# Fourier mixing and GEGLU: gate and value of every third late block in two TensorE passes each, with the mirrored gelu, the value add and the product issued a slot later

## The chip, the cores and the metric

One core of a Trainium2 chip. The time is that of one execution on the device, in microseconds, median of several. TensorE (PE), VectorE (DVE), ScalarE (ACT) and GpSimd (POOL) each work through a queue of their own in order, and wait for one another by semaphores. TensorE's sums go into the memory PSUM (tiles `ps_...` of the profile), from which DVE and ACT read them; tiles `..._sb` lie in SBUF, the core's other memory.

## The reference, cut to what matters

```python
X = np.fft.fft(np.fft.fft(x, axis=1), axis=2).real       # x: 8 x 3008 x 256
g, val = X @ w_gate, X @ w_val                           # 256 -> 1536
out = (0.5 * g * (1 + erf(g / sqrt(2))) * val) @ w_out   # 1536 -> 256
```

The real part of a transform of real data is mirrored: a row and its mirror row have the same part E and an odd part O of opposite sign. So with the products E and O of one row, its gate is E + O and that of the mirror row E - O. One column of E does not fit the halves and is added as a rank-one term: the row EB times a weight `yw`.

## The kernel before: the parts that matter

It goes through 288 blocks (8 batches, 3 chunks of 512, 512 and 481 tokens, 12 feature blocks `fc`). A turn of the loop is a **slot**: the first half of one block, the second half of the block before, and two pieces of the output product of the chunk before.

```python
def l1_gate(ci, fc):                       # three gate passes in all: E, O, then M = -2 O
    pg = psum("g")
    mm(pg, n, "g", "E", fs, E, True, False)
    mm(pg, n, "g", "O", fs, O, False, True)
    nc.scalar.activation(gl[:, 0, :n], pg[:, :n], AF.Gelu)          # row
def l1_gate2(ci, fc):                      # a slot later
    mm(pg, n, "g", "M", fs, O, False, True, skip_group_check=True)
    nc.scalar.activation(<gl[:, 1], mirrored>, pg[:, :n], AF.Gelu)  # mirror row
def l1_value(ci, fc):                      # two value passes: E, O
    mm(pv, n, "v", "E", fs, E, True, True)
    nc.vector.scalar_tensor_tensor(ve, EB, yw, pv, op0=mult, op1=add)
def l1_value2(ci, fc):                     # a slot later
    mm(pv, n, "v", "O", fs, O, False, True, skip_group_check=True)
    nc.vector.tensor_tensor(h[0], gl[0], pv, op=mult)
    nc.vector.scalar_tensor_tensor(<vv, mirrored>, ve, 2.0, pv, op0=mult, op1=subtract)
    nc.gpsimd.tensor_tensor(h[1], gl[1], vv, op=mult)
# ... one slot of the loop:
    G(i); g(i - 1); V(i); <output piece>; <input folds>; v(i - 1); <output piece>; <transform work>
```

(Cut and shortened.)

## Time and profile before

| before | |
|---|---|
| median of the runs beside the first result | 630.28 us (629.87 to 631.15) |
| span of the profiled run | 627.0 us |
| PE, DVE, POOL, ACT busy | 98%, 92%, 81%, 68% |
| one slot at 512 columns | 1.955 us |

"Busy" is the share of the span in which an engine has an instruction in work. PE's 98% says that it is hardly ever without work, and the chain says that it sets the time. The prediction below shows the page's lines and one slot of the timeline.

### The profile page before, as it was taken

What the parts mean: (1) busy time and instruction counts of PE and PEld (TensorE: products, weight loads), DVE (VectorE), ACT (ScalarE), POOL (GpSimd) and SP (SyncE); (2) the same over time, 40 slices, a digit from 0 to 9 for tenths busy, and PEclk for the clock granted to TensorE, in tenths of its full rate; (3) what the DMA queues carried; (4) which work ended last, traced back from release to release, by engine and by line L of the source; (5) the groups of instructions that cost most, each with busy time, mean ns of one, the idle gap of its engine ahead of it and who ended that gap; (6) DMA issues with size and microseconds to landing.
All of it is one profiled execution on the core that took longest, in us unless ns stands there. A gap on an engine that the chain in (4) does not pass through costs nothing.

```text
span 627.0 us, 12895 instructions
## 1 busy us (share of the span) xinstructions
PE 612.3 (98%) x4195; PEld 405.1 (65%) x4243; DVE 578.3 (92%) x941; ACT 428.4 (68%) x842; POOL 505.3 (81%) x510
## 2 busy tenths in 40 slices
PE   7999999999999999999999999999999999999997
PEld 3456666666666666666666666666666666666666
DVE  8689989999899999999999998999999999999992
ACT  6777677666776677667676677676676666666661
POOL 8399999989897998879997899969988655555651
PEclk8999999999999999999999999999999999999999
DMA  9961754536353353731645335633212322221123
GB/s 177 227 97 31 210 129 116 144 105 159 99 146 101 98 133 79 184 113 46 160 110 135 101 78 127 148 97 98 62 49 63 91 86 55 51 52 39 42 51 81
DMA packets 54217, 65.40 MB, mean 104 GB/s; under 512 B 7831, under 2 KB 49802, under 8 KB 51754
## 3 DMA queue, kind: packets, MB, share of 16 engines
q1 hardware_dynamic: 47222, 49.03, 30.6%
q0 software_dynamic: 6608, 15.29, 11.4%
q8 instruction: 33, 0.54, 0.4%
q10 hardware_dynamic: 320, 0.26, 0.2%
q14 instruction: 34, 0.28, 0.2%
HBM read 39.65 MB, written 30.17 MB: 111 GB/s over the span
## 4 chain that ended last, share of the span: by engine, by line
PE 93%; ACT 2%; issue 1%; DVE 1%; DMA 1%; POOL 1%; POOLq 0%; ACTq 0%
PE ps_o L749 38%; PE ps_g L660 28%; PE ps_v L660 19%; PE ps_dft L546 2%; PE ps_dft L582 2%; PE ps_o L820 1%; DMA Z_sb<-z 1%; PE ps_dft L443 1%; PE ps_dft L612 0%; ACT gelu_sb L676 0%; POOL h_sb L724 0%; POOL eo_sb L224 0%; DMA out_dram<-out_sb 0%; ACT gelu_sb L685 0%; PE ps_dft L749 0%
## 5 line engine op out<-in xcount | busy, mean ns | idle before, releaser
L724 POOL TENSOR_TENSOR h_sb<-gelu_sb,v_sb 128x512 bf16<-128x512 bf16 (+1 forms) x280 | 319.8, 1146 | 93.1 <-DVE v_sb L722 85.9
L749 PE MATMUL ps_o<-Wo_sb,h_sb 128*128 128x256 bf16 (+1 forms) x2232 | 334.9, 273 | 0.9 <-POOL h_sb L724 0.9
L749 PEld LDWEIGHTS <-h_sb 128*128 128x128 bf16 (+1 forms) x2304 | 228.7, 100 | 112.9 <-POOL h_sb L724 2.6
L676 ACT ACTIVATE gelu_sb<-ps_g 128x512 bf16<-128x512 f32 (+1 forms) x288 | 169.4, 588 | 98.6 <-PE ps_g L660 80.9
L660 PE MATMUL ps_g<-EO_sb,W_sb 128*128 128x512 bf16 (+1 forms) x817 | 228.5, 375 | 3.8 <-ACT gelu_sb L685 0.8
L704 DVE SCALAR_TENSOR_TENSOR ve_sb<-EB_sb,yw,ps_v 128x512 f32<-128x512 bf16 (+1 forms) x280 | 206.3, 737 | 25.9 <-PE ps_v L660 25.0
L660 PE MATMUL ps_v<-EO_sb,W_sb 128*128 128x512 bf16 (+1 forms) x575 | 213.7, 375 | 0.7 <-DVE W_sb L451 0.6
L720 DVE TENSOR_TENSOR h_sb<-gelu_sb,ps_v 128x512 bf16<-128x512 bf16 (+1 forms) x280 | 189.9, 678 | 1.1 <-ACT gelu_sb L685 0.7
L660 PEld LDWEIGHTS <-W_sb 128*128 128x128 bf16 x1440 | 137.2, 98 | 81.1 <-issue 1.8
L722 DVE SCALAR_TENSOR_TENSOR v_sb<-ve_sb,ps_v 128x512 f32<-128x512 f32 (+1 forms) x280 | 187.5, 670 | 0.0
L685 ACT ACTIVATE gelu_sb<-ps_g 128x512 bf16<-128x512 f32 (+1 forms) x288 | 168.7, 586 | 0.0
L769 ACT ACTIVATE out_sb<-ps_o 128x512 f32<-128x512 f32 x92 | 55.0, 598 | 35.7 <-PE ps_o L749 35.6
L224 POOL TENSOR_TENSOR eo_sb<-ab_sb 94x512 bf16<-94x512 f32 (+1 forms) x70 | 77.6, 1111 | 0.5
L549 ACT ACTIVATE S_sb<-ps_dft 96x512 bf16<-96x512 f32 x56 | 32.9, 588 | 14.0 <-PE ps_dft L546 13.9
L592 ACT ACTIVATE EO_sb<-ps_dft 128x512 bf16<-128x512 f32 (+1 forms) x44 | 26.0, 590 | 23.3 <-PE ps_dft L582 22.1
L217 POOL TENSOR_TENSOR ab_sb<-x_raw,x_raw 94x508 f32<-94x508 f32 (+1 forms) x30 | 33.0, 1100 | 0.0
L220 POOL TENSOR_TENSOR ab_sb<-x_raw,x_raw 94x508 f32<-94x508 f32 (+1 forms) x30 | 32.9, 1098 | 0.0
L546 PE MATMUL ps_dft<-eo_sb,G 94*96 94x256 bf16 x119 | 22.5, 274 | 0.2 <-POOL eo_sb L224 0.2
L158 POOL DMA_INDIRECT x_raw<-in_x_dram,idx x18 | 17.1, 948 | 2.9 <-issue 1.1
L582 PE MATMUL ps_dft<-TP,Z_sb 128*128 128x128 bf16 (+1 forms) x184 | 17.8, 218 | 0.0
L582 PEld LDWEIGHTS <-Z_sb 128*128 128x128 bf16 x192 | 14.6, 98 | 1.8 <-DVE Z_sb L534 0.6
L546 PEld LDWEIGHTS <-G 94*96 94x96 bf16 x119 | 13.0, 123 | 1.2 <-issue 0.4
(148 smaller groups left out, 166.2 us busy)
## 6 DMA issues: line engine op xcount, KB each, us to landing
out_dram<-out_sb SPq DMA_DIRECT2D x364, 64.0 KB
x_raw<-in_x_dram SPq DMA_DIRECT2D x10, 768.0 KB
Z_sb<-z SPq DMA_DIRECT2D x7, 768.0 KB
z<-S_sb SPq DMA_DIRECT2D x7, 576.0 KB
EB_sb<-yrow SPq DMA_DIRECT2D x14, 128.0 KB
z<-S_sb SPq DMA_DIRECT2D x7, 192.0 KB
x_raw<-in_x_dram SPq DMA_DIRECT2D x2, 640.0 KB
EB_sb<-yrow SPq DMA_DIRECT2D x7, 120.2 KB
```

The costliest lines, as they stand in the source:

```text
L224: eng.tensor_tensor(_sub(eo, [[C, nj], [1, 128]], j0 * C + g * 128), ab(0, 0, [[1, 128]]), ab(1, 0, [[1, 128]]), op=op)
L546: nc.tensor.matmul(ps[:96, q * C : (q + 1) * C], G[:, j, :], _sub(eo, [[1, C]], j * C), start=(j == js[0]), stop=(j == js[-1]))
L582: nc.tensor.matmul(ps[:, o : o + n], st["Z"][:, pair, g * 128 : g * 128 + 128], _sub(TP, [[1, n]], g * 128), start=True, stop=True)
L660: nc.tensor.matmul(ps[:, :n], W[nm, part][:, fs], src, start=start, stop=stop, **kw)
L676: nc.scalar.activation(gl[:, 0, :n], pg[:, :n], AF.Gelu)
L685: nc.scalar.activation(_sub(gl, [[-1, n]], TOK + n - 1), pg[:, :n], AF.Gelu)
L704: nc.vector.scalar_tensor_tensor(ve[:, :n], EB_bufs[b][:, c0 : c0 + n], yw[:, fc : fc + 1], pv[:, :n], op0=ALU.mult, op1=ALU.add)
L720: nc.vector.tensor_tensor(st["h"][:, fc, 0, :n], gl[:, 0, :n], pv[:, :n], op=ALU.mult)
L722: nc.vector.scalar_tensor_tensor(_sub(vv, [[-1, n]], n - 1), ve[:, :n], 2.0, pv[:, :n], op0=ALU.mult, op1=ALU.subtract)
L724: nc.gpsimd.tensor_tensor(st["h"][:, fc, 1, :n], gl[:, 1, :n], vv[:, :n], op=ALU.mult)
L749: nc.tensor.matmul(pso[:m, half], st["h"][:, fc, sign, h0 : h0 + m], Wo_sb[:, fc, :], start=(fc == 0 and not (first and sign)), stop=(fc = ...
L769: nc.scalar.activation(_sub(osb, [[1, 2 * C]], 0, part_num=m), pso[:m, :], AF.Copy)
```

## The change

Its intent is to use the time that POOL and ACT have free in the last sixty blocks (41% and 36% between 543 and 590 us) to take one pass from PE. In nineteen blocks (229, 232, ... 283) ACT copies twice the E product out of PSUM, before the O pass is added to it. The mirror row is then (2 E) - (E + O), a subtraction, and the M pass is not needed. In the diff `d` holds the gate of the mirror row while it is made. To keep DVE at three instructions a block, the value goes the same way: the copy takes the place of `ve`.

```diff
+APART = tuple(i for i in range(B * NS - 60, B * NS - 2) if i % 3 == 1)
+def e2_tile(): return work([128, TOK], FP32, "e2", 2, "e2_sb")       # two buffers
 def l1_gate:
+    if apart(ci, fc):
+        mm(pg, n, "g", "E", fs, E, True, True)
+        nc.scalar.activation(e2[:, :n], pg[:, :n], AF.Copy, scale=2.0)
+def l1_gate_odd:                                # same slot, after the first output piece
+    mm(pg, n, "g", "O", fs, O, False, True, skip_group_check=True)
+    nc.vector.scalar_tensor_tensor(d, EB, ywg, pg, op0=mult, op1=subtract)
+    nc.scalar.activation(gl[:, 0, :n], pg[:, :n], AF.Gelu)
+    nc.gpsimd.tensor_tensor(d, e2, d, op=add)                        # "gate add"
 def l1_value:
+    if apart(ci, fc):
+        nc.scalar.activation(e2[:, :n], pv[:, :n], AF.Copy, scale=2.0)  # "value copy"
 def l1_value2:
+    if apart(ci, fc):
+        nc.vector.scalar_tensor_tensor(<vv, mirrored>, EB, yw2, pv, op0=mult, op1=subtract)
+        def rest():
+            nc.scalar.activation(<gl[:, 1], mirrored>, d, AF.Gelu)
+            nc.gpsimd.tensor_tensor(vv, <e2, mirrored>, vv, op=add)  # "value add"
+            nc.gpsimd.tensor_tensor(h[1], gl[1], vv, op=mult)
+        late.append(rest)                       # issued in the next slot, behind v(i)
```

(Cut and shortened. Left out: the weights `ywg` and `yw2`, made once, and a fifth `v` buffer.)

More of the change, by code (lines that the diff above doesn't have):

```diff
@@ L134, in v_tile, with e2_tile @@
     def v_tile():
-        return work([128, TOK], FP32, "v", 4, "v_sb")
+        return work([128, TOK], FP32, "v", 5, "v_sb")
+    def e2_tile():
+        return work([128, TOK], FP32, "e2", 2, "e2_sb")
     def osb_tile():
@@ L245 @@
     one_h = const_pool.tile([1, 1], BF16)
-    yw = const_pool.tile([128, NFC], FP32)
+    yw, yw2, ywg = (const_pool.tile([128, NFC], FP32, name=f"yw_{i}") for i in range(3))
     NGP = NJ * NK
@@ L250 @@
     rd = work([128, 2 * NGP + NK], FP32, "Z", 1, "rd")
-    cf, cr, cd = (work([128, C], FP32, t, 4, f"small_{i}") for i, t in enumerate(("v", "v", "v")))
+    cf, cr, cd = (work([128, C], FP32, t, 5, f"small_{i}") for i, t in enumerate(("v", "v", "v")))
     tf, tr, td = (work([128, 128], FP32, t, 3, f"small_t{i}") for i, t in enumerate(("ve", "ve", "ve")))
@@ L477, in make_yw, with make_ywg @@
         return run
+    def make_ywg():
+        fcs = sorted({i % NFC for i in APART})
+        ps = psum("dft")
+        for fc in fcs:
+            nc.tensor.matmul(
+                ps[:, fc : fc + 1], W["g", "O"][0:1, fc * 128 : (fc + 1) * 128], one_h, start=True, stop=True)
+        for fc in fcs:
+            nc.scalar.activation(ywg[:, fc : fc + 1], ps[:, fc : fc + 1], AF.Copy, scale=2.0)
+        nc.vector.tensor_scalar(yw2, yw, 2.0, None, op0=ALU.mult)
     EO_bufs, EB_bufs = {}, {}
@@ L634, in tp_o @@
         return tp_e(b, gi, 1, engine)
+    NS = NG * NFC
+    APART = tuple(i for i in range(B * NS - 60, B * NS - 2) if i % 3 == 1)
     def store(b, gi, sub, sign, osb_half, queue):
@@ L654, in store @@
             (nc.sync if i else queue).dma_start(out=dst, in_=_sub(osb_half, [[1, C]], 0, part_start=p1, part_num=hi - lo))
+    late = []
     def ffn_work(b):
@@ L667, in cols_of, with apart @@
             return n, c0, E, O, cstate[ci], slice(fc * 128, (fc + 1) * 128)
+        def apart(ci, fc):
+            return b * NS + ci * NFC + fc in APART
         def l1_gate(ci, fc):
@@ L672, in run @@
                 pg = psum("g")
+                if apart(ci, fc):
+                    mm(pg, n, "g", "E", fs, E, True, True)
+                    e2 = e2_tile()
+                    nc.scalar.activation(e2[:, :n], pg[:, :n], AF.Copy, scale=2.0)
+                    st["ps"][fc] = [pg, gelu_tile(), e2]
+                    return
                 mm(pg, n, "g", "E", fs, E, True, False)
@@ L678, in l1_gate, with l1_gate_odd, run @@
             return run
+        def l1_gate_odd(ci, fc):
+            def run():
+                if not apart(ci, fc):
+                    return
+                n, c0, _, O, st, fs = cols_of(ci, fc)
+                pg, gl, e2 = st["ps"][fc][:3]
+                del st["ps"][fc][2]
+                mm(pg, n, "g", "O", fs, O, False, True, skip_group_check=True)
+                d = v_tile()
+                nc.vector.scalar_tensor_tensor(
+                    d[:, :n], EB_bufs[b][:, c0 : c0 + n], ywg[:, fc : fc + 1], pg[:, :n],
+                    op0=ALU.mult, op1=ALU.subtract)
+                nc.scalar.activation(gl[:, 0, :n], pg[:, :n], AF.Gelu)
+                nc.gpsimd.tensor_tensor(d[:, :n], e2[:, :n], d[:, :n], op=ALU.add)
+                st["ps"][fc][0] = d
+            return run
         def l1_gate2(ci, fc):
@@ L683, in run @@
                 pg, gl = st["ps"][fc][:2]
+                if apart(ci, fc):
+                    return
                 mm(pg, n, "g", "M", fs, O, False, True, skip_group_check=True)
@@ L702, in run @@
                 mm(pv, n, "v", "E", fs, E, True, True)
+                if apart(ci, fc):
+                    e2 = e2_tile()
+                    nc.scalar.activation(e2[:, :n], pv[:, :n], AF.Copy, scale=2.0)
+                    st["ps"][fc] += [pv, e2]
+                    return
                 ve = ve_tile()
@@ L711, in run @@
             def run():
-                n, _, _, O, st, fs = cols_of(ci, fc)
-                _, gl, pv, ve = st["ps"].pop(fc)
+                n, c0, _, O, st, fs = cols_of(ci, fc)
+                dg, gl, pv, ve = st["ps"].pop(fc)
                 if three(ci, fc):
@@ L721, in run @@
                 vv = v_tile()
+                if apart(ci, fc):
+                    nc.vector.scalar_tensor_tensor(
+                        _sub(vv, [[-1, n]], n - 1), EB_bufs[b][:, c0 : c0 + n], yw2[:, fc : fc + 1], pv[:, :n],
+                        op0=ALU.mult, op1=ALU.subtract)
+                    def rest():
+                        nc.scalar.activation(_sub(gl, [[-1, n]], TOK + n - 1), dg[:, :n], AF.Gelu)
+                        nc.gpsimd.tensor_tensor(vv[:, :n], _sub(ve, [[-1, n]], n - 1), vv[:, :n], op=ALU.add)
+                        nc.gpsimd.tensor_tensor(st["h"][:, fc, 1, :n], gl[:, 1, :n], vv[:, :n], op=ALU.mult)
+                    late.append(rest)
+                    return
                 nc.vector.scalar_tensor_tensor(
@@ L777, in ffn_work @@
             parts = {k: [f(ci, fc) for fc in range(NFC)] for k, f in (
-                ("G", l1_gate), ("V", l1_value), ("g", l1_gate2), ("v", l1_value2))}
+                ("G", l1_gate), ("O", l1_gate_odd), ("V", l1_value), ("g", l1_gate2), ("v", l1_value2))}
             subs = [nsub - 1, *range(nsub - 1)] if last(ci) else range(nsub)
@@ L874, in behind_first_gate @@
         tp_y(0, 0)()
-    NS = NG * NFC
     def plan():
@@ L894, in plan @@
             at(fill, s, f)
+        at(fill, 14, make_ywg)
         for i, f in enumerate(early):
@@ L972, in feed @@
                 two.pop(0)()
+            parts["O"][fc]()
             for f in pool.pop(i, []):
                 f()
+            ready = list(late)
+            late.clear()
             if before:
                 before[0]["v"][before[1]]()
+            for f in ready:
+                f()
             if two:
```

## The prediction

> **What bounds the kernel now.** I read the page from the top: busy shares first, then the forty slices, then the chain that ended last.
>
> ```profile
> PE 612.3 (98%) x4195; PEld 405.1 (65%) x4243; DVE 578.3 (92%) x941; ACT 428.4 (68%) x842; POOL 505.3 (81%) x510
> ...
> POOL 8399999989897998879997899969988655555651
> ...
> PE 93%; ACT 2%; issue 1%; DVE 1%; DMA 1%; POOL 1%; POOLq 0%; ACTq 0%
> ```
>
> TensorE holds 93% of the chain. POOL runs near full until the input folds are over, then falls to about half in the last slices. That hole is what the change spends. The changed blocks are numbers 229, 232, ... 283 of 288 (nineteen), and by counting the starts of the ve instruction (L704) in the timeline backwards they lie between 496 and 604 us. So I read that stretch by windows (columns: length, then busy time of PE, weight load, DVE, ACT, POOL; clock; DMA):
>
> ```profile
> 543.00:590.00 47.00, 46.68 (x309) 30.94 (x313) 46.99 (x73) 30.08 (x57) 27.94 (x25) 1.00 0.18 44
> 590.00:611.00 21.00, 21.00 (x146) 14.01 (x144) 20.91 (x34) 12.93 (x26) 12.44 (x12) 1.00 0.21 51
> ```
>
> PE and DVE are both full there, ACT and POOL have 36 to 41% free. One block in the timeline (start, length, engine):
>
> ```profile
> 559.66 0.38 PE L660 MATMUL ps_g<-EO_sb,W_sb 128*128 128x512 bf16 x1
> ...
> 559.88 0.38 PE L660 MATMUL ps_v<-EO_sb,W_sb 128*128 128x512 bf16 x1
> ...
> 560.29 0.75 DVE L704 SCALAR_TENSOR_TENSOR ve_sb<-EB_sb,yw,ps_v 128x512 f32<-128x512 bf16 x1
> 560.41 0.59 ACT L685 ACTIVATE gelu_sb<-ps_g 128x512 bf16<-128x512 f32 x1
> ...
> 560.49 1.16 POOL L724 TENSOR_TENSOR h_sb<-gelu_sb,v_sb 128x512 bf16<-128x512 bf16 x1 [0.79 <-DVE v_sb L722]
> 560.53 0.38 PE L660 MATMUL ps_v<-EO_sb,W_sb 128*128 128x512 bf16 x1
> ...
> 561.02 0.69 DVE L720 TENSOR_TENSOR h_sb<-gelu_sb,ps_v 128x512 bf16<-128x512 bf16 x1
> ...
> 561.62 0.68 DVE L722 SCALAR_TENSOR_TENSOR v_sb<-ve_sb,ps_v 128x512 f32<-128x512 f32 x1
> 561.83 0.38 PE L660 MATMUL ps_v<-EO_sb,W_sb 128*128 128x512 bf16 x1
> ```
>
> A slot lasts 1.955 us (the same value pass starts at 559.88 and 561.83). It holds nine times 0.217 us of PE: gate E, O and M, value E and O, and two output pieces of four 256-column passes, each piece worth two. DVE has no gap, but it is not at its floor: where it is behind, early in the run, the same three instructions start 0.60, 0.60 and 0.65 apart, 1.85 in all:
>
> ```profile
> 45.81 0.68 DVE L722 SCALAR_TENSOR_TENSOR v_sb<-ve_sb,ps_v 128x512 f32<-128x512 f32 x1
> 46.41 0.74 DVE L704 SCALAR_TENSOR_TENSOR ve_sb<-EB_sb,yw,ps_v 128x512 f32<-128x512 bf16 x1
> 47.06 0.68 DVE L720 TENSOR_TENSOR h_sb<-gelu_sb,ps_v 128x512 bf16<-128x512 bf16 x1
> ```
>
> So PE is the bound, with DVE 5% behind.
>
> **What the Trainium skill says.** "TensorE: Matmul & The Clock Gate", Back-to-back issue gap, gives N/2.4 + 2.5 ns: 216 ns for 512 columns; the trace has 217. "GPSIMD Engine Reference", Elementwise side-by-side cycle accounting, gives about 2.6 cycles an element for two inputs (1.11 us for 512 at its 1.2 GHz); the trace has the product at 1.166 us, started every 1.12 when back to back. "PSUM — Partial Sum Buffer", bank collisions, says two engines may not use one bank at once, readers included; in the order of the changed kernel the first gelu of a changed block does wait for the DVE subtraction that reads the same gate bank (no run here has shown a collision). "Perfetto Trace Analysis", Optimization Strategy, says that a gap which repeats can mean too few buffers; the trace of before has no such gap on PE, and I expect one after.
>
> **The change part by part.** Per changed block:
> - PE loses the M gate pass: 0.217 us at 512 columns, 0.204 at 481. Twelve and seven blocks: 12 x 0.217 + 7 x 0.204 = 4.0 us, all on the path. This is the most that can be won (0.6%).
> - ACT gains two copies PSUM to SBUF (e2 of gate, e2 of value) at 0.60 us like the output copy L769: 23 us in a stretch with 36% free.
> - DVE keeps three instructions: ve becomes the gate subtraction, and the mirrored value takes a pointer scalar like L704, so about 0.06 us more per block.
> - POOL gains two fp32 adds. The folds L217 and L220 with two fp32 inputs take 1.26 us at 508 columns and start 1.22 apart. Three slots then hold 3 x 1.12 + 2 x 1.23 = 5.8 us of POOL: that alone nearly eats the three slots (3 x 1.955 - 0.217 = 5.65).
> - Once, in slot 14: four one-column passes, four small ACT copies, one DVE instruction; a similar copy takes 0.18 us. About 0.3 us.
>
> Sums do not decide, order does. Queues are in order, and I read them from the two programs. e2 has two buffers, one copy for the gate and one for the value in each changed block i, so **the value copy of block i+3 must wait for the POOL add that reads the value copy of block i.** The program's waits show it: that copy has a POOL wait from the second changed block on, and none in the first. That add is issued a slot late, and on POOL it stands behind the plain product of block i+1. PE's value O pass of block i+3 then needs the copy. This closes a ring, which I follow from E, the end of the value copy of block i (512 columns):
> - ACT: the first gelu of block i comes next, ends E+0.49 (spacing of ACT). PE's value O pass of i starts about E+0.05. DVE's product of i starts at about E+0.50.
> - DVE in order: mirrored value of i (+0.60), ve of i+2 (+0.66), product of i+1 (+0.66), mirrored value of i+1 (+0.60), which ends +0.68 later: E+3.70. I add 0.05 because the second gelu of i+1 may hold its product: E+3.75.
> - POOL starts 0.14 after (560.35 to 560.49 above): product of i+1 1.12, then the late add of i 1.26: E+6.27.
> - ACT starts about 0.10 later and copies for 0.60: E+6.97.
> The ring takes **7.0 us per three slots, against 5.87 before**. At 481 columns the same sum is 0.46+3.05+0.05+0.14+1.06+1.19+0.10+0.57 = 6.62, say 6.65, against 5.67.
>
> Between the nineteen blocks lie eighteen such intervals: ten at 512, five at 481, three mixed (6.85). 10 x 7.0 + 5 x 6.65 + 3 x 6.85 = 123.8 us. Before, ve of block 229 starts at 496.33 and of block 283 at 602.92: 106.6 us, with the transform work of the last batch in it, which the new waits can hide. **Difference +17.2 us.** Add 0.3 for slot 14 and 0.4 because POOL's last products end later behind the late adds. Together 630.6 + 17.9 = **648.5 us** (+2.8%).
>
> **The rivals.**
> 1. PE stays the bound and the pass is saved: 630.6 - 4.0 + 0.3 = 627. For it speaks that PE carries the chain and ACT and POOL have room by share; against it the ring above, 1.3 us longer than PE's new 5.65.
> 2. POOL is the bound by sheer work: 5.8 to 5.95 us per three slots against 5.87 before, so 629 to 633, the same. Holds if the copy's wait is satisfied early, that is if POOL got to the late add about a slot sooner than I think.
> 3. A slower ring without the buffers: gate subtraction, DVE, product, late add, late product, next gate add, late gelu, next gate copy, PE's gate O pass. By the same spacings it takes about 12.2 us per two intervals, 6.1 each, plus up to 1.8 us at four chunk ends where output pieces need the late product of the eleventh block: 634 to 638. It is what remains if the e2 wait binds less.
> 4. Contention of POOL and DVE: in 100 to 400 us POOL is about 90% busy and DVE's durations are the same as in the tail, so I give it nothing.
>
> **Range and chances.** The ring has three terms that I estimate: fp32 add on 128 partitions (plus or minus 0.1 us), the hand-offs (0.1) and whether a product waits for a second gelu (0.14). With eighteen intervals, 0.15 us more or less moves the total by 2.7 us; two of them 5 us. So 642 to 654. The 2% line is at 643.2, so slower by over 2% is at 0.87; within 2% takes rivals 1 to 3, at 0.12; faster by over 2% would need 12.4 us where 4.0 is all there is: 0.01.
>
> **What would show it.** Right: from about 500 us on PE idles once per three slots for about 1.2 us, just before the value O pass of a changed block (one slot after its gate), and the releaser is the ACT copy to e2; that copy's own idle time ends by POOL's add of v; changed blocks recur about every 7.0 us at 512 columns; POOL's share there rises to about 80%, PE's falls to about 80%; the time up to 495 us is unchanged. Wrong if the copy is found waiting for PE only, if the POOL add takes under 1.0 us, or if PE has no gaps there. If PE's gaps stand before the gate O pass or before output pieces, it is rival 3.

## The result, and the profile after

The changed kernel takes 648.63 us (647.56 to 651.10, four runs), before 630.28. Ratios are the mean time of one kernel's fast runs over that of the other's of the same rounds, so not quite the ratio of the medians: 1.0295 (95% interval 1.0263 to 1.0326), slower.

The same lines of the page, after:

```profile
PE 613.8 (95%) x4180; PEld 403.6 (62%) x4228; DVE 578.7 (89%) x942; ACT 446.2 (69%) x884; POOL 548.7 (85%) x548
...
PE   7999999999999999999999999999999888887887
...
POOL 8399999899897999789987999789986778888882
...
PE 75%; ACT 8%; issue 7%; DVE 4%; POOL 3%; DMA 2%; SPq 0%; ACTq 0%; POOLq 0%; DVEq 0%
```

PE falls to 8 tenths in just the slices where POOL rises. PE's part of the chain drops from 93% to 75%; ACT, DVE and POOL now hold stretches of it. No engine is full there: by windows (length, then busy PE, weight load, DVE, ACT, POOL), the changed kernel's plain middle of the changed blocks is

```profile
543.00:590.00 47.00, 40.23 (x260) 25.79 (x264) 40.02 (x63) 32.05 (x64) 38.84 (x35) 1.00 0.19 41
```

PE 86%, DVE 85%, POOL 83%, ACT 68%, clock 1.00. When no engine is full, the question is who waits for whom. The list of waits between 480 and 632 us names it (engine, line, what it waited for: total, times, longest; the value copy is L755, the value add L784; the profile calls the e2 tiles e_sb):

```profile
ACT e_sb L755 <- POOL v_sb L784: 36.4, 18, 2.7
...
PE ps_v L682 <- ACT e_sb L755: 16.9, 18, 1.6
```

Eighteen times, which is the number of intervals between nineteen changed blocks, the value copy waits for the value add, and eighteen times PE waits for the copy. One turn of the ring in the timeline (start, length, engine):

```profile
589.95 0.60 ACT L755 ACTIVATE e_sb<-ps_v 128x512 f32<-128x512 f32 x1 [2.19 <-POOL v_sb L784]
...
590.60 0.38 PE L682 MATMUL ps_v<-EO_sb,W_sb 128*128 128x512 bf16 x1 [1.13 <-ACT e_sb L755]
...
591.08 0.69 DVE L775 TENSOR_TENSOR h_sb<-gelu_sb,ps_v 128x512 bf16<-128x512 bf16 x1 [0.65 <-ACT gelu_sb L723]
...
593.64 0.68 DVE L789 SCALAR_TENSOR_TENSOR v_sb<-ve_sb,ps_v 128x512 f32<-128x512 f32 x1
...
594.47 1.16 POOL L791 TENSOR_TENSOR h_sb<-gelu_sb,v_sb 128x512 bf16<-128x512 bf16 x1 [0.96 <-DVE v_sb L789]
...
595.59 1.26 POOL L784 TENSOR_TENSOR v_sb<-e_sb,v_sb 128x512 f32<-128x512 f32 x1
...
596.89 0.60 ACT L755 ACTIVATE e_sb<-ps_v 128x512 f32<-128x512 f32 x1 [2.18 <-POOL v_sb L784]
```

Read it downwards. The copy lands, PE starts the value O pass 0.05 us later, DVE works off five instructions (the first and the last are shown), POOL makes the product of the next block (L791) and only then the add (L784), and the next copy starts 0.04 us after the add ends. From copy to copy it is 6.94 us, where three slots took 5.87. The engine with the gap (PE) is not the one to blame, and neither is the one that it waits for (ACT, which idles 2.18 us itself).

### The profile page after: what moved, and what is told of

It is laid out like the page before. It is cut to its first block, busy times and chain, and to the rows that moved or that the text cites. A ratio compares the mean times of both kernels' runs of the same rounds, so it can differ in the third digit from the quotient of the medians.

```text
span 647.0 us, 12945 instructions
## 1 busy us (share of the span) xinstructions
PE 613.8 (95%) x4180; PEld 403.6 (62%) x4228; DVE 578.7 (89%) x942; ACT 446.2 (69%) x884; POOL 548.7 (85%) x548
## 4 chain that ended last, share of the span: by engine, by line
PE 75%; ACT 8%; issue 7%; DVE 4%; POOL 3%; DMA 2%; SPq 0%; ACTq 0%; POOLq 0%; DVEq 0%
PE ps_o L816 30%; PE ps_g L682 23%; PE ps_v L682 16%; POOL v_sb L784 3%; ACT gelu_sb L707 2%; PE ps_dft L560 2%; DVE v_sb L789 2%; ACT gelu_sb L735 1%; PE ps_dft L596 1%; ACT gelu_sb L723 1%; DMA out_dram<-out_sb 1%; ACT out_sb L836 1%; DMA Z_sb<-z 1%; DMA EB_sb<-yrow 1%; DVE h_sb L775 1%
## 5 line engine op out<-in xcount | busy, mean ns | idle before, releaser
L791 POOL TENSOR_TENSOR h_sb<-gelu_sb,v_sb 128x512 bf16<-128x512 bf16 (+1 forms) x261 | 297.8, 1145 | 68.8 <-DVE v_sb L789 63.1
L682 PE MATMUL ps_g<-EO_sb,W_sb 128*128 128x512 bf16 (+1 forms) x798 | 226.9, 375 | 4.8 <-ACT gelu_sb L735 1.1
L682 PE MATMUL ps_v<-EO_sb,W_sb 128*128 128x512 bf16 (+1 forms) x575 | 213.7, 375 | 18.0 <-ACT e_sb L755 16.9
L759 DVE SCALAR_TENSOR_TENSOR ve_sb<-EB_sb,yw,ps_v 128x512 f32<-128x512 bf16 (+1 forms) x261 | 192.1, 736 | 25.1 <-PE ps_v L682 23.7
L707 ACT ACTIVATE gelu_sb<-ps_g 128x512 bf16<-128x512 f32 (+1 forms) x269 | 158.6, 589 | 71.3 <-PE ps_g L682 57.0
L682 PEld LDWEIGHTS <-W_sb 128*128 128x128 bf16 x1421 | 135.3, 97 | 79.2 <-issue 4.5
L789 DVE SCALAR_TENSOR_TENSOR v_sb<-ve_sb,ps_v 128x512 f32<-128x512 f32 (+1 forms) x261 | 174.7, 669 | 0.0
L735 ACT ACTIVATE gelu_sb<-ps_g 128x512 bf16<-128x512 f32 (+1 forms) x269 | 157.9, 587 | 0.0
L836 ACT ACTIVATE out_sb<-ps_o 128x512 f32<-128x512 f32 x92 | 55.1, 598 | 28.1 <-PE ps_o L816 27.8
L755 ACT ACTIVATE e_sb<-ps_v 128x512 f32<-128x512 f32 (+1 forms) x19 | 11.2, 588 | 36.4 <-POOL v_sb L784 36.4
L724 POOL TENSOR_TENSOR v_sb<-e_sb,v_sb 128x512 f32<-128x512 f32 (+1 forms) x19 | 23.7, 1247 | 0.0
L785 POOL TENSOR_TENSOR h_sb<-gelu_sb,v_sb 128x512 bf16<-128x512 bf16 (+1 forms) x19 | 21.7, 1141 | 1.5
L720 DVE SCALAR_TENSOR_TENSOR v_sb<-EB_sb,yw,ps_g 128x512 f32<-128x512 bf16 (+1 forms) x19 | 14.0, 736 | 9.9 <-PE ps_g L682 9.9
```

Source lines behind the costliest of these rows:

```text
L682: nc.tensor.matmul(ps[:, :n], W[nm, part][:, fs], src, start=start, stop=stop, **kw)
L735: nc.scalar.activation(_sub(gl, [[-1, n]], TOK + n - 1), pg[:, :n], AF.Gelu)
L759: nc.vector.scalar_tensor_tensor(ve[:, :n], EB_bufs[b][:, c0 : c0 + n], yw[:, fc : fc + 1], pv[:, :n], op0=ALU.mult, op1=ALU.add)
L789: nc.vector.scalar_tensor_tensor(_sub(vv, [[-1, n]], n - 1), ve[:, :n], 2.0, pv[:, :n], op0=ALU.mult, op1=ALU.subtract)
L791: nc.gpsimd.tensor_tensor(st["h"][:, fc, 1, :n], gl[:, 1, :n], vv[:, :n], op=ALU.mult)
L836: nc.scalar.activation(_sub(osb, [[1, 2 * C]], 0, part_num=m), pso[:m, :], AF.Copy)
```

## The experiments

My theory: the value copy needs one of two e2 buffers, the buffer is freed by the late value add, and the add stands behind the product of block i+1 on POOL. Rivals: POOL's amount of work is the bound (A), the buffers are all there is to it (B), lateness as such costs the time (C), or each changed block brings a fixed cost. All kernels gave correct results; a run of before took 1299 us; it is in no ratio.

### Four buffers for the copies

```diff
-work([128, TOK], FP32, "e2", 2, "e2_sb")
+work([128, TOK], FP32, "e2", 4, "e2_sb")
```

> Four buffers for the e2 copies in place of two, nothing else. My ring (the value copy of block i+3 waits for the late POOL add of block i, which stands behind the product of block i+1): the wait of that copy on POOL, 36.4 us in the changed kernel, falls to under 3 us; the time falls to the next ring, which I put at 6.1 us per interval plus chunk ends, so 634 to 638 us; the gaps of TensorE move to the gate O pass and to output pieces. Rival A (POOL's work is the bound, whatever the buffers): stays at 645 to 649. Rival B (the buffers are all there is to it): 627 to 630.

638.63 us against 630.20, ratio 1.0127 (1.0112 to 1.0142). Ten of the eighteen microseconds are gone with the wait, which is not among the waits any more. PE's gaps now stand in two other places (from its timeline):

```profile
561.56 0.38 PE L682 MATMUL ps_g<-EO_sb,W_sb 128*128 128x512 bf16 x1 [0.43 <-ACT e_sb L701]
567.73 0.38 PE L682 MATMUL ps_g<-EO_sb,W_sb 128*128 128x512 bf16 x1 [0.36 <-ACT e_sb L701]
573.96 0.38 PE L682 MATMUL ps_g<-EO_sb,W_sb 128*128 128x512 bf16 x1 [0.29 <-ACT e_sb L701]
577.75 0.39 PE L816 MATMUL ps_o<-Wo_sb,h_sb 128*128 128x256 bf16 x2 [1.24 <-POOL h_sb L785]
```

Gate O passes (L682, waiting for the gate copy L701) come every 6.2 us, and at each of the four chunk ends an output piece waits 1.24 to 1.31 us for a late product (L785). So rival A is out as the cause of the whole, and so is B: behind the first ring stands a second, rival 3 of the prediction, which put it at 6.1. My 634 to 638 was 0.6 us low.

### The value add on time

```diff
         nc.vector.scalar_tensor_tensor(<vv, mirrored>, EB, yw2, pv, op0=mult, op1=subtract)
+        nc.gpsimd.tensor_tensor(vv, <e2, mirrored>, vv, op=add)
         def rest():
             nc.scalar.activation(<gl[:, 1], mirrored>, d, AF.Gelu)
-            nc.gpsimd.tensor_tensor(vv, <e2, mirrored>, vv, op=add)
             nc.gpsimd.tensor_tensor(h[1], gl[1], vv, op=mult)
```

> Two e2 buffers as in the changed kernel, but the POOL add of the value is issued right behind the DVE instruction that feeds it; the mirrored gelu and the product stay a slot late. My ring: the copy's buffer comes free about 3 us sooner, its wait on POOL falls to under 3 us in all, and as the add also leaves the queue ahead of the next gate add, the second ring is broken too (5.5 us per interval); POOL's work of 5.8 to 5.9 us per interval remains, with about 0.5 us at four chunk ends: 630 to 634. Rival A (POOL's work alone made the 18 us): stays at 645 to 649, for the work is the same. Rival C (the late gelu and product are the cause): stays above 640.

629.55 us, ratio 0.9985 (0.9970 to 1.0001): the eighteen microseconds are gone by moving one POOL instruction a slot forward, with two buffers and the same work. The same move takes the add out of the second ring, where it stood ahead of the late product and the next gate add; so it gives back more than four buffers did. The copy still waits for POOL, 3.0 us in six times (under 3 was expected), but PE no longer waits for the copy. POOL does more in the same time, not less:

```profile
543.00:590.00 47.00, 45.78 (x302) 30.01 (x307) 45.86 (x74) 38.70 (x73) 45.74 (x41) 1.00 0.20 45
```

POOL is 97% busy here, against 83% in the slow kernel, so its work did not set the slow kernel's time (rival A). It is near full only now, and so are PE and DVE (97% and 98%); which of them holds the time of this run is not shown. Rival C falls as well: gelu and product are still late. Of PE's gaps three chunk ends are left, 0.19 to 0.81 us. The time came out just under my 630 to 634.

### Every sixth block

```diff
-if i % 3 == 1)
+if i % 6 == 1)
```

> Ten changed blocks in place of nineteen, every sixth. My ring: a copy has twice the time to get its buffer back (11.7 us, needs 7), so no wait at all: each block saves its 0.21 us, 630.3 - 2.1 + 0.3 to 1.0 = 628.5 to 629.3. A cost that each changed block brings with it (18.3 us / 19 = 0.97 us a block, ten blocks): 640. POOL as the bound: about half full there, no bound, as my ring.

628.55 us, ratio 0.9968 (0.9956 to 0.9980). No wait of a copy on POOL is among the waits. The ten changed blocks save 1.65 us, where ten passes are worth 2.1, so no fixed cost near the 0.97 us a block shows: the cost lies in the distance between two of them. With six slots the copy has its buffer in time.

### No changed block

```diff
-if i % 3 == 1)
+if i % 3 == 1)[:0]
-fcs = sorted({i % NFC for i in APART})
+fcs = [1, 4, 7, 10]
```

> No changed block, but the preparation kept (four one-column passes, four small ACT copies, one DVE instruction, the fifth v buffer). I said 0.3 us for it; the two profiles are 0.7 to 1.2 us apart ahead of the first changed block. So 630.5 if the 0.3 holds, up to 631.4 if that shift belongs to it and is not spread of the start-up.

630.19 us, ratio 1.0001 (0.9988 to 1.0013). The preparation costs nothing that five rounds show. So the lead of about 1 us that the two profiles had before block 229 belongs to spread. The other profiles agree: in the eight runs with changed blocks the first gate copy starts anywhere from 495.63 to 499.10 us, after the same work.

### The copies in bf16

```diff
-work([128, TOK], FP32, "e2", 2, "e2_sb")
+work([128, TOK], BF16, "e2", 2, "e2_sb")
```

> The changed kernel with the e2 copies stored as bf16, nothing else. An add with one bf16 input should take about 1.15 us in place of 1.27 (before: 1.145 with bf16 inputs, 1.26 with fp32). My ring holds one of the two adds, so 0.11 us less per interval, 18 intervals: 2 us off the changed kernel, 646.6. If POOL's sum were the bound both adds count: 4 us off, 644.6. If neither: 648.6.

647.12 us (645.41 to 649.83), ratio 1.0273 to before; beside the 1.0295 of the changed kernel, the intervals of the two overlap, so the total does not decide between the expectations. The trace does, for it has the same ring turn after turn:

```profile
563.97 0.38 PE L682 MATMUL ps_v<-EO_sb,W_sb 128*128 128x512 bf16 x1 [1.02 <-ACT e_sb L755]
570.80 0.38 PE L682 MATMUL ps_v<-EO_sb,W_sb 128*128 128x512 bf16 x1 [1.02 <-ACT e_sb L755]
577.63 0.38 PE L682 MATMUL ps_v<-EO_sb,W_sb 128*128 128x512 bf16 x1 [1.02 <-ACT e_sb L755]
```

Here it is 6.83 us a turn, 6.94 in the changed kernel (562.65 to 569.59). Both adds became shorter by 0.11 us (1.27 to 1.16) and the ring by 0.11: it holds one of the two, as I had it. If POOL's sum set the pace, it would be 0.22. The turns at 481 columns tell the two adds apart. There only the gate add became shorter (1.21 to 1.11), the value add did not (1.03 and 1.04), and neither did the turn: 6.52 us here, 6.50 in the changed kernel (617.49 to 623.99); the other four agree within 0.01. So the add in the ring is the value add.

```profile
618.06 0.58 ACT L755 ACTIVATE e_sb<-ps_v 128x481 bf16<-128x481 f32 x1 [1.90 <-POOL v_sb L784]
624.58 0.58 ACT L755 ACTIVATE e_sb<-ps_v 128x481 bf16<-128x481 f32 x1 [1.89 <-POOL v_sb L784]
```

### The gate alone

```diff
 l1_value:   -the value copy; ve on DVE as in plain blocks
 l1_value2:  -scalar_tensor_tensor(<vv, mirrored>, EB, yw2, pv, op0=mult, op1=subtract)
             +scalar_tensor_tensor(<vv, mirrored>, ve, 2.0, pv, op0=mult, op1=subtract)
 rest:       -the value add
```

> The changed kernel with the gate part alone: value as in plain blocks (ve on DVE), gate in two passes with copy, DVE subtraction, POOL add, late gelu and late product. No value copy, so no ring through it. DVE has ten instructions per interval in place of nine: 3 x 1.85 + 0.66 = 6.2 us at 512 columns against 5.87 before, 5.95 at 481 against 5.67; with the stretch that holds transform work giving slack, about +4 us, and up to 3 at chunk ends: 633 to 637, DVE full, waits of the value copy absent. If the value copy is not needed for the 18 us: 645 or more.

634.45 us, ratio 1.0061 (1.0042 to 1.0081), as expected. There is no value copy and no 18 us. What is left is DVE's tenth instruction, and its window is full (46.98 of 47.00 us busy):

```profile
543.00:590.00 47.00, 44.75 (x291) 28.91 (x296) 46.98 (x77) 32.13 (x63) 35.79 (x32) 1.00 0.20 43
```

The late value add is gone here too, so this run takes away the whole ring and not the copy alone. This is why the change moved the value as well, and why it needed the copy at all.

### Nothing late

```diff
-late.append(rest)
+rest()
```

(on top of "the value add on time")

> The add, the mirrored gelu and the product all issued as in plain blocks, nothing late. The mirrored gelu then stands in ACT's queue ahead of the output copy and of the next gelu, and waits for POOL's gate add, which comes about 0.3 us or more after it; I expect gaps before output pieces of about 0.3 us per interval: 632 to 636. If lateness itself made the 18 us: 630 or below.

637.27 us, ratio 1.0120 (1.0103 to 1.0137), a microsecond above my 632 to 636. The place of the gaps is as expected, their size 0.47 to 0.66 us at eleven of seventeen places and not 0.3:

```profile
582.26 0.63 ACT L784 ACTIVATE gelu_sb<-v_sb 128x512 bf16<-128x512 f32 x1 [0.75 <-POOL v_sb L724]
...
582.80 0.58 ACT L836 ACTIVATE out_sb<-ps_o 128x512 f32<-128x512 f32 x1
...
583.43 0.60 PE L816 MATMUL ps_o<-Wo_sb,h_sb 128*128 128x256 bf16 x4 [0.64 <-ACT out_sb L836]
```

The mirrored gelu waits for the gate add (L724) and holds up the output copy L836 behind it, and PE waits for that. So the slot of delay for the gelu and the product is worth 8 us (637.27 against 629.55); only the add must not share it.

### A version that beats both

```diff
-if i % 3 == 1)
+if i % 3 == 1 and i % NFC != 10)
```

(on top of "the value add on time": the eleventh block of each chunk, whose late product held up the chunk ends, stays plain)

> The add on time, and the eleventh block of each chunk left plain (fifteen changed blocks). In the run with the add on time what is left are gaps of 0.2 to 0.8 us at chunk ends before output pieces, by the late product of that block, and a POOL that is 97% busy. Both go: 15 x 0.21 = 3.2 us saved of 630.2: 627.0, up to 628.3 if POOL still holds it in parts.

626.66 us (625.16 to 629.75), ratio 0.9952 (0.9931 to 0.9974): half a per cent faster than the kernel before and about 3% faster than the changed one. Fifteen passes at 0.21 us are 3.2 us, and 3.4 us is what the medians show. In the stretch of the changed blocks PE has no gap. A fixed four-buffer version with the add on time was not run: with the add on time PE waits for no copy.

## Why the prediction was right, point by point

- **Size.** 648.5 was predicted, 648.63 measured; slower by over 2% had 0.87.
- **The ring.** From the end of one copy (590.55) the trace has: DVE's product at +0.53 (I had 0.50), the mirrored value of block i+1 done at +3.77 (3.75), the add done at +6.30 (6.27), the copy done at +6.94 (6.97). The hand-off from POOL to ACT was 0.04 us, not 0.10, and the small excesses before it make up for it. At 481 columns I had 6.65 for all; the turns last 6.50 to 6.93, although the value add took 1.03 us there and not my 1.19, so that sum has other terms too small.
- **The sum.** Counted on PE, from the value O pass of block 229 to that of block 283, the eighteen intervals take 125.1 us (499.53 to 624.62), before 106.5 (498.52 to 605.05): 18.6 us more, where I had 17.2. Seventeen of them, from PE's first gap (506.99) to its last (624.62), make 17.0 of it. The first interval makes the other 1.6, with 7.46 us for 5.87. (From copy to copy it is 8.46, because the first copy waits for nobody and so comes early.) The last product holds PE up for 0.74 us where it was 0.30: the 0.4 us I had put in.
- **Terms that were off.** The preparation, put at 0.3 us, costs nothing that can be measured. I made no allowance for the long first interval, nor for the turns of 7.38 and 7.17 us around the first change of chunk length. So the ring's sum was 1.4 us short. The two profiled runs lie 20.0 us apart (627.0 and 647.0), 1.0 of it spread ahead of block 229, and the medians 18.35. That the total came within 0.2 us of the median is partly luck; the ring and the length of its plain turn (6.94, 6.97 predicted) are not.
- **POOL's share.** I expected about 80% for POOL and for PE; the window has 83% and 86%.
- **The rivals.** Rival 1 (only the pass is saved, 627) is what the change is worth once the waits are out: 626.66 with fifteen blocks. Rival 2 (POOL full, 629 to 633) fits the run with the add on time, 629.55, where POOL is 97% busy, though PE and DVE are as full. Rival 3 (the second ring, 634 to 638) is the run with four buffers, 638.63. Rivals 1 and 3 were not false, they stood in a row behind the ring: each shows when what stands before it is taken away. Rival 4 had no part: DVE's durations are the same in all runs (L789 and L722: 0.68 us).
- **From the skill.** A gap that repeats can mean too few buffers ("Perfetto Trace Analysis", Optimization Strategy). Four buffers did remove the wait, and so the page agrees with this trace, yet they gave back only ten of eighteen microseconds. The order of the queue gave back all. As for the PSUM bank that two readers share: with four buffers the first gelu waits eighteen times, 7.4 us in all, for the DVE subtraction that reads the same bank, and no run shows a collision.

## What to carry to other kernels

Free time of an engine is not enough to take work; ask where in its queue the new instruction will stand, and which buffer it frees. Follow one buffer from writer to last reader and back to its next writer, add up what stands ahead of each step on its engine, and compare the sum with the time between two uses: here 7 us stood against 5.65. When you delay something, delay only what must wait, and leave on time the instruction that frees a buffer.

## What the Trainium skill lacked or had wrong

- "TensorE: Matmul & The Clock Gate", Back-to-back issue gap: the formula that the prediction took from it, 216 ns for 512 columns, is called there the gap of an isolated matmul; for a stream of weight loads and matmuls the section has about 131 ns. This kernel is such a stream, and its slot of nine passes shows 217 ns a pass.
- "GPSIMD Engine Reference", Elementwise side-by-side cycle accounting: one figure for two inputs, about 2.6 cycles an element (an estimate from it: 1.11 us for 512). The runs show a dependence on the type of the inputs that it lacks: two fp32 inputs of 128x512 take 1.27 us, one bf16 and one fp32 1.16.
- The same section: the value add (one input read backwards) took 1.267 us at 512 columns and 1.034 at 481, 18% less for 6% fewer columns (from its start to that of the next instruction 1.35 and 1.11), with fp32 and bf16 copies alike (1.039), while the gate add (both forwards) took 1.270 and 1.206. No page has it, and no run here tells why.
- "Perfetto Trace Analysis", Per-engine timelines, names the step in which a semaphore update travels to the other engines, but gives no duration for the compute engines. Here the hand-offs are DVE to POOL 0.14 to 0.15 us, POOL to ACT 0.04, ACT to PE 0.05, by the profile's starts and ends.
